# Block 0 of a sliding-window attention layer: values copied from SBUF to SBUF, or written to DRAM once and read back

## The chip, the cores and the metric

The kernel runs on one core of a Trainium2 chip. The core has five engines, each with its own queue of instructions in a fixed order: TensorE (PE, matmuls), VectorE (DVE), ScalarE (ACT), GpSimd (POOL) and SyncE (SP), which here issues the transfers. The transfers themselves are carried out by 16 DMA engines. SBUF is the core's memory of 128 partitions, PSUM the accumulators that PE writes, DRAM the chip's large memory. The metric is the time of one launch on the device, in microseconds (us), as the median of several runs.

## The reference

Four layers follow one another, A, B, A, B, on a sequence of 2048 positions with 512 features, 32 heads of 16. Each adds its result to x. Layer A is linear attention with a softmax feature map. Layer B, which the change touches, is attention over 8 earlier positions, two apart:

```python
W, dil = 8, 2
idx = pos[:, None] - off[None, :]          # off = 0, 2, ..., 14
kg = k[:, :, idx_c, :]                     # 8 keys for each position
vg = v[:, :, idx_c, :]                     # 8 values for each position
logits = einsum("bhsd,bhswd->bhsw", q, kg) * scale   # masked where idx < 0
attn = softmax(logits, axis=-1)
o = einsum("bhsw,bhswd->bhsd", attn, vg)   # then @ wo
```

x = x + A(layernorm(x)) and x = x + B(layernorm(x)), each twice, with the same weights the second time. All data are bf16.

## The kernel before, in words

The 2048 positions are worked on in four blocks of 512, b = 0 to 3. x stays in SBUF from beginning to end. A layer is a row of stages for each block, and the stages of different blocks, and of neighbouring layers, are interleaved, so that block 1 of a layer may be ahead of block 0.

Layer B of one block goes like this. The normalised x (xn) is transposed to xnT, with features on the partitions; for most blocks this is one DMA transpose that SP issues (line 451, "xnT<-xn"). Stage b1 (s_b1) multiplies xnT with WB (line 928) into q, k and v; four PSUM tiles each are copied to SBUF as QT, K and V (line 192 by ACT or line 190 by DVE). K and V have a rim of 16 columns with the last positions of the block before, which POOL copies (lines 954 to 970). Stage b2 forms the products of q with the eight shifted k (line 1026, DVE), sums them over the features of a head by matmuls with a 0/1 matrix (line 1033, PE), takes the exponential (line 1040, ACT), and sums and divides (lines 1049 to 1061). Stage b3 multiplies the attention weights PT with the values (pav, line 1088, DVE), sums over the window by matmuls (line 1097) and multiplies with the output weights WoB (line 520); lines 523 to 533 add x.

In the b3 stage the partitions stand for window offset and head, not for features. So V, which has features on the partitions, has to be spread: for each of the four feature groups dl = 0 to 3 and each of four window offsets g, a set of 32 rows of V (one for each head) is copied to the 32 partitions from 32 g on, each copy with its columns shifted by 2 g. The result is Vg, one tile for two dl. That makes sixteen copies of 32 rows (131.5 KB each) for a block. They are issued by vrep, one step for each dl, four copies in a step (line 995).

For b = 1, 2, 3 the step for dl = 0 first issues vwr (line 974): the whole V tile of the block is written to a DRAM buffer "vd" (528 KB), and the sixteen copies read from there ("Vg<-vd"). A copy can only be issued when the write has landed, so SP waits there. For b = 0 there is no write, and the copies read the V tile in SBUF itself ("Vg<-V").

The order in which each engine does its steps is written out by hand as one long list (_ORDER) of step names; _CHOICE says which copies go to DVE and which to ACT, and _SLOTS which buffer each tile gets. SP therefore issues its transfers in one fixed order, and an issue that waits holds all issues behind it. Each transfer takes the next of eight completion counters in turn, and its issue waits until the transfer before it on that counter has landed.

In SP's order, around the first layer B, stand: the first four copies of block 0; the write and the first four read-backs of block 1; the transpose of block 2; the other twelve read-backs of block 1; the transpose of block 3; the other twelve copies of block 0; the write of block 2 and its read-backs. In the second layer B stand: the transpose of block 1; eight copies of block 0; the transpose of block 2; the other eight copies of block 0; the transpose of block 3; then write and read-backs of block 1.

Of the kernel before, what the change touches and what calls it, by code (L numbers as in the profile page):

```python
# [19 lines left out]
H = 32  # L20
# [3 lines left out]
NB = 4  # L24
# [5 lines left out]
KVW = 16 + TB  # L30
VGW = 3 * KVW + TB + 8
# [98 lines left out]
class _Fast:  # L130
# [789 lines left out]
    def s_b1(self, L, b):  # L920
        nc, add = self.nc, self.step
        st = "b1_%d%d" % (L, b)
        T = {}
        def mm(i, c):
            xnT = self.xnT["B%d" % L, b]
            T[i, c] = pp = self.ps()
            for k in range(NB):
                nc.tensor.matmul(pp[:], lhsT=self.WB[:, k, i * D + c:(i + 1) * D:NB], rhs=xnT[:, :, k, :],  # L928
                                 start=(k == 0), stop=(k == NB - 1))

        def ev(i, c, dve):
            if i == 0:
                if (L, b) not in self.QT:
                    self.QT[L, b] = self.med([NB, TB], "QT")
                dst = self.QT[L, b][:, c, :]
            elif i == 1:
                ktile()
                dst = self.K[L, b][:, c, 16:KVW]
            else:
                vtile()  # L940
                dst = T["V"][:, c, 16:KVW]
            self.copy(dve, dst, T[i, c][:])

        def ktile():
            if (L, b) not in self.K:
                self.K[L, b] = self.med([NB, KVW], "K")

        def vtile():
            if "V" not in T:
                T["V"] = self.med([NB, KVW], "V")  # L950

        def halo():
            ktile()
            nc.gpsimd.tensor_copy(out=self.K[L, b][:, :, 0:16], in_=self.K[L, b - 1][:, :, TB:KVW])

        def kzero():
            ktile()
            nc.gpsimd.memset(self.K[L, b][:, :, 0:16], 0.0)

        def vzero():  # L960
            vtile()
            nc.gpsimd.memset(T["V"][:, :, 0:16], 0.0)

        def vhalo_in():
            vtile()
            nc.gpsimd.tensor_copy(out=T["V"][:, :, 0:16], in_=self.vh[L, b - 1][:])

        def vhalo_out():
            self.vh[L, b] = self.sm([NB, 16], "vh", BF16)
            nc.gpsimd.tensor_copy(out=self.vh[L, b][:], in_=T["V"][:, :, TB:KVW])  # L970

        def vwr():
            self.VD[L, b] = self.dram.tile([P, NB * KVW], BF16, name="vd%d%d" % (L, b))
            nc.sync.dma_start(out=self.VD[L, b][:], in_=T["V"][:].rearrange("p c t -> p (c t)"))

        def vrep(dl):
            if dl == 0:
                self.Vg[L, b] = {}
            if dl % 2 == 0:
                self.Vg[L, b][dl // 2] = self.big([2, NB * KVW], "Vg")  # L980
            if (L, b) in _OPT["v_dram"]:
                a = self.VD[L, b][dl:dl + 1, 2:3]
                src = bass.AP(a.tensor, a.offset, [[2, 4], [4 * NB * KVW, H], [1, VGW]])
                nc.sync.dma_start(out=self.Vg[L, b][dl // 2][:, dl % 2, 0:VGW], in_=src)
                return
            if dl == 0 and b:
                vwr()
            for g in (0, 2, 1, 3):
                if b:
                    a = self.VD[L, b][dl:dl + 1, 2 + 2 * g:3 + 2 * g]  # L990
                    src = bass.AP(a.tensor, a.offset, [[4 * NB * KVW, H], [1, VGW]])
                else:
                    a = T["V"][dl:dl + 1, 0:1, 2 + 2 * g:3 + 2 * g]
                    src = bass.AP(a.tensor, a.offset, [[4 * a.ap[0][0], H], [1, VGW]])
                nc.sync.dma_start(out=self.Vg[L, b][dl // 2][32 * g:32 * g + 32, dl % 2, 0:VGW], in_=src)

        if b:
            add(st + "v", "POOL", vhalo_in)
        else:
            add(st + "k", "POOL", kzero)  # L1000
            add(st + "v", "POOL", vzero)
        for i in range(3):
            for c in range(NB):
                add(st + "qkv"[i], "PE", mm, i, c)
                self.flex(st + "qkv"[i], ev, i, c)
        if b:
            add(st + "kh", "POOL", halo)
        if b < 3:
            add(st + "v", "POOL", vhalo_out)
        if (L, b) in _OPT["v_dram"]:  # L1010
            add(st + "v", "SP", vwr)
        for dl in range(4):
            add(st + "v", "SP", vrep, dl)
# [232 lines left out]
class _Layout:  # L1246
# [6 lines left out]
    def add(self, name, nelem, nbuf=1):  # L1253
        self.regions[name] = (self.off, nelem, nbuf)
        self.off += nelem * nbuf
        return self
# [568 lines left out]
```

## Time and profile before

| | |
|---|---|
| median of 3 runs | 327.89 us (327.71 to 328.19) |
| profiled execution | 328.31 us, its span 326.6 us |
| busy share of the span | PE 95%, DVE 93%, ACT 86%, POOL 8% |
| chain that ended last | PE 81%, ACT 8%, DMA 5%, DVE 3% |
| copies Vg<-V (block 0) | 32 of 131.5 KB, median 4.4 us to landing |
| copies Vg<-vd (blocks 1 to 3) | 96 of 131.5 KB, median 3.0 us to landing |
| writes vd<-V | 6 of 528.0 KB, median 3.1 us to landing |
| granted PE clock | 0.999 of full |

The profile comes from one execution, whose time (328.31 us) is a little above the median of the runs. Its span of 326.6 us begins with the first and ends with the last instruction; what lies around it belongs to the launch. PE and DVE are both busy nearly all the time, so the share of busy time alone doesn't say which of them sets the end at a given place. The chain does: it is followed back from the last instruction, at each step to what released it. "Line L928" is line 928 of the kernel. PEld is PE's loading of weights, which runs beside the matmuls.

In a list in order of time each row has its start and its length in us, the engine, and the operation; for SP the length is the time that the issuing took, not that of the transfer. "DMA to landing" is the time from issue until the data are there.

### The profile page before, as it was taken

What the parts mean: (1) busy time and instruction counts of PE and PEld (TensorE: products, weight loads), DVE (VectorE), ACT (ScalarE), POOL (GpSimd) and SP (SyncE); (2) the same over time, 40 slices, a digit from 0 to 9 for tenths busy, and PEclk for the clock granted to TensorE, in tenths of its full rate; (3) what the DMA queues carried; (4) which work ended last, traced back from release to release, by engine and by line L of the source; (5) the groups of instructions that cost most, each with busy time, mean ns of one, the idle gap of its engine ahead of it and who ended that gap; (6) DMA issues with size and microseconds to landing.
All of it is one profiled execution on the core that took longest, in us unless ns stands there. A gap on an engine that the chain in (4) does not pass through costs nothing.

```text
span 326.6 us, 8036 instructions
## 1 busy us (share of the span) xinstructions
PE 309.8 (95%) x3176; PEld 149.7 (46%) x3203; DVE 302.2 (93%) x439; ACT 279.2 (86%) x634; POOL 25.4 (8%) x50
## 2 busy tenths in 40 slices
PE   7999999999999999999999999979999999989873
PEld 3655456445454444443444455644544554433220
DVE  7998995998999999999989999699999999999993
ACT  5999988998898999899999999798999996676550
POOL 4000000000021002000000000000000208400000
PEclk9999999999999999999999999999999999999999
DMA  7980000014557889687540200042336976468632
GB/s 200 364 211 4 0 2 4 2 29 120 118 136 181 211 152 133 190 143 188 151 132 13 54 3 2 4 121 75 99 67 123 173 164 197 143 219 248 186 118 85
DMA packets 39404, 38.92 MB, mean 119 GB/s; under 512 B 24256, under 2 KB 33472, under 8 KB 39360
## 3 DMA queue, kind: packets, MB, share of 16 engines
q1 hardware_dynamic: 38832, 38.32, 47.3%
q8 instruction: 27, 0.44, 0.6%
q14 instruction: 17, 0.14, 0.2%
q10 hardware_dynamic: 528, 0.02, 0.1%
HBM read 23.43 MB, written 5.87 MB: 90 GB/s over the span
## 4 chain that ended last, share of the span: by engine, by line
PE 81%; ACT 8%; DMA 5%; DVE 3%; SPq 1%; issue 1%; DVEq 0%
PE ps L928 24%; PE ps L520 15%; PE ps L593 9%; PE ps L605 8%; PE ps L698 6%; PE ps L1097 4%; PE ps L1033 3%; ACT oT L192 3%; PE ps L668 2%; PE ps L460 2%; ACT Eq L706 2%; DMA xnT<-xn 2%; DMA wraw<-in_A_wqkv_dram 1%; PE ps L523 1%; PE ps L901 1%
## 5 line engine op out<-in xcount | busy, mean ns | idle before, releaser
L928 PE MATMUL ps<-xnT,WB 128*128 128x512 bf16 x384 | 87.5, 380 | 0.1
L1026 DVE TENSOR_TENSOR prod<-QT,K 128x4096 bf16<-128x4096 bf16 x32 | 72.5, 2290 | 0.3 <-ACT QT L192 0.2
L1088 DVE TENSOR_TENSOR pav<-PT,Vg 128x4096 bf16<-128x4096 bf16 (+1 forms) x34 | 72.0, 2161 | 0.4
L928 PEld LDWEIGHTS <-WB 128*128 128x128 bf16 x384 | 42.5, 114 | 42.6 <-issue 5.8
L520 PEld LDWEIGHTS <-oT 128*128 128x128 bf16 x256 | 23.9, 98 | 34.4 <-ACT oT L192 5.8
L192 ACT CAST oT<-ps 128x512 bf16<-128x512 f32 (+1 forms) x60 | 32.1, 586 | 8.4 <-PE ps L1097 7.0
L706 ACT ACTIVATE Eq<-ps 128x512 bf16<-128x512 f32 x64 | 34.0, 614 | 0.7 <-PE ps L698 0.5
L520 PE MATMUL ps<-WoB,oT 128*128 128x512 bf16 x122 | 32.1, 380 | 2.4 <-ACT oT L192 2.0
L599 ACT ACTIVATE Ek<-ps 128x512 bf16<-128x512 f32 x64 | 33.6, 621 | 0.3 <-PE ps L593 0.2
L698 PE MATMUL ps<-xnT,WA 128*128 128x512 bf16 x128 | 30.6, 380 | 0.6 <-DVE Eq L816 0.6
L540 ACT ACTIVATE sqd<-x 128x512 bf16<-128x512 bf16 x48 | 30.1, 643 | 0.5 <-DVE x L533 0.3
L593 PE MATMUL ps<-WA,xnT 128*128 128x512 bf16 x124 | 29.7, 379 | 0.8 <-DMA xnT<-xn 0.5
L605 PE MATMUL ps<-WA,xnT 128*128 128x512 bf16 x120 | 30.0, 379 | 0.5 <-issue 0.2
L520 PE MATMUL ps<-WoA,oT 128*128 128x512 bf16 x120 | 29.2, 379 | 0.4
L533 DVE SCALAR_TENSOR_TENSOR x<-ps,x 128x512 bf16<-128x512 f32 x38 | 25.3, 685 | 2.5 <-PE ps L520 2.4
L192 ACT CAST V<-ps 128x512 bf16<-128x512 f32 x31 | 17.5, 597 | 4.4 <-PE ps L928 4.3
L192 ACT CAST K<-ps 128x512 bf16<-128x512 f32 x31 | 17.9, 587 | 3.5 <-PE ps L928 3.4
L530 ACT ACTIVATE x<-ps 128x512 bf16<-128x512 f32 x26 | 15.2, 600 | 6.3 <-PE ps L523 6.3
L593 PEld LDWEIGHTS <-xnT 128*128 128x128 bf16 x128 | 12.1, 98 | 15.6 <-DMA xnT<-xn 0.9
L192 ACT CAST QT<-ps 128x512 bf16<-128x512 f32 x29 | 17.1, 592 | 2.5 <-PE ps L928 2.5
L651 DVE TENSOR_TENSOR Ek<-Ek,rk 128x4096 bf16<-128x4096 bf16 (+1 forms) x10 | 18.6, 1858 | 0.5 <-ACT rk L646 0.5
L446 ACT ACTIVATE xn<-x,nmr,rstd 128x512 bf16<-128x512 bf16 x23 | 18.2, 822 | 0.8 <-DVE nmr L435 0.6
(129 smaller groups left out, 433.2 us busy)
## 6 DMA issues: line engine op xcount, KB each, us to landing
Vg<-vd SPq DMA_DIRECT2D x96, 131.5 KB, 3.0
Vg<-V SPq DMA_DIRECT2D x32, 131.5 KB, 4.4
Prho<-rd SPq DMA_DIRECT2D x8, 512.0 KB, 5.1
vd<-V SPq DMA_DIRECT2D x6, 528.0 KB, 3.1
x<-in_A_x_dram SPq DMA_DIRECT2D x3, 512.0 KB, 6.8
WB<-in_B_wqkv_dram SPq DMA_DIRECT2D x3, 512.0 KB, 10.9
wraw<-in_A_wqkv_dram SPq DMA_DIRECT2D x4, 256.0 KB, 4.3
out_dram<-x SPq DMA_DIRECT2D x4, 256.0 KB, 2.3
```

The source lines that it names most:

```text
L192: self.nc.scalar.copy(out=out, in_=in_)
L520: nc.tensor.matmul(y[:], lhsT=oT[:, c, t * P:(t + 1) * P], rhs=Wo()[:, c, :], start=(c == 0), stop=(c == NB - 1 and not onpe))
L533: nc.vector.scalar_tensor_tensor(out=xb[:, t, :], in0=T[t][:], scalar=1.0, in1=xb[:, t, :], op0=ALU.mult, op1=ALU.add, **kw)
L540: nc.scalar.activation(out=sqd[:], in_=xb[:, t, :], func=ACT.Square, accum_out=T["ss"][:, t:t + 1])
L593: nc.tensor.matmul(pk[:], lhsT=xnT[:, t, k, :], rhs=self.WA[:, k, D:2 * D], start=(k == 0), stop=(k == NB - 1))
L599: nc.scalar.activation(out=T["E"][:, t, s, :], in_=T["k", t][:], func=ACT.Exp, scale=1.0 - 2.0 * s)
L605: nc.tensor.matmul(pv[:], lhsT=xnT[:, t, k, :], rhs=self.WA[:, k, 2 * D:3 * D], start=(k == 0), stop=(k == NB - 1))
L698: nc.tensor.matmul(pq[:], lhsT=self.WA[:, k, hb * P:(hb + 1) * P], rhs=xnT[:, :, k, :], start=(k == 0), stop=(k == NB - 1))
L706: nc.scalar.activation(out=self.Eq[L, b][s][:, :, hb, :], in_=T[hb][:].rearrange("p (t i) -> p t i", t=4), func=ACT.Exp, scale=1.0 - 2.0 * s)
L928: nc.tensor.matmul(pp[:], lhsT=self.WB[:, k, i * D + c:(i + 1) * D:NB], rhs=xnT[:, :, k, :], start=(k == 0), stop=(k == NB - 1))
L1026: nc.vector.tensor_tensor(out=pr[:], in0=QT[:, c:c + 1, :].to_broadcast([P, NW, TB]), in1=win, op=ALU.mult)
L1088: nc.vector.tensor_tensor(out=pv, in0=PT[:, :, lo:lo + n].unsqueeze(1).to_broadcast([P, NB, 2, n]), in1=vw, op=ALU.mult)
```

## The change: block 0 goes through DRAM too

In vrep, block 0 is treated as the other blocks are: its step for dl = 0 first writes the V tile to a DRAM buffer of its own, and all sixteen copies read that buffer. This holds for both layers B. The order of the steps, the buffers and the engines of all other work stay the same.

```diff
@@ def vrep(dl), in s_b1
-            if dl == 0 and b:
+            if dl == 0:
                 vwr()
             for g in (0, 2, 1, 3):
-                if b:
-                    a = self.VD[L, b][dl:dl + 1, 2 + 2 * g:3 + 2 * g]
-                    src = bass.AP(a.tensor, a.offset, [[4 * NB * KVW, H], [1, VGW]])
-                else:
-                    a = T["V"][dl:dl + 1, 0:1, 2 + 2 * g:3 + 2 * g]
-                    src = bass.AP(a.tensor, a.offset, [[4 * a.ap[0][0], H], [1, VGW]])
+                a = self.VD[L, b][dl:dl + 1, 2 + 2 * g:3 + 2 * g]
+                src = bass.AP(a.tensor, a.offset, [[4 * NB * KVW, H], [1, VGW]])
                 nc.sync.dma_start(out=self.Vg[L, b][dl // 2][32 * g:32 * g + 32, dl % 2, 0:VGW], in_=src)
```

SP has two issues more (one write in each layer B); 32 copies change their source from SBUF to DRAM. The write function that vrep calls is this:

```python
def vwr():
    self.VD[L, b] = self.dram.tile([P, NB * KVW], BF16, name="vd%d%d" % (L, b))
    nc.sync.dma_start(out=self.VD[L, b][:], in_=T["V"][:].rearrange("p c t -> p (c t)"))
```

## The prediction, made before the changed kernel was timed

> **What bounds the kernel now.** I read three views: the page's engine shares and its chain, then the chain in order of time, then SP's queue in order of time. First the page: TensorE (PE) is busy for 95% of the span and carries 81% of the chain that ended last.
>
> ```profile
> span 326.6 us, 8036 instructions
> PE 309.8 (95%) x3176; PEld 149.7 (46%) x3203; DVE 302.2 (93%) x439; ACT 279.2 (86%) x634; POOL 25.4 (8%) x50
> PE 81%; ACT 8%; DMA 5%; DVE 3%; SPq 1%; issue 1%; DVEq 0%
> ```
>
> The change touches layer B, which runs twice: from about 84 to 150 us, and from 238 us to the end. The chain in order of time (start, length, what), from the first of them:
>
> ```profile
> 107.69 1.41 PE ps L1033 x24
> 109.09 1.85 PE ps L928 x8
> ...
> 134.00 5.32 PE ps L928 x24
> 139.34 0.59 ACT K L192
> ...
> 140.97 1.41 ACT xn L446 x2
> 142.41 5.73 DMA xnT<-xn
> 148.14 0.05 issue
> 148.19 0.39 PE ps L593
> ```
>
> The reader is to see that from 107.69 to 139.3 the chain has matmuls alone, one behind another, then a short piece of ACT, one transpose by DMA, and PE again. So a moment that PE loses at 109 is not made good before 148: each of these steps begins when the one before it ends. The rows left out are of the same kind.
>
> SP issues every transfer, in one fixed order, and an issue that waits holds all that stand behind it. Its queue (start, time in issue, line, what) in the stretch of the first block 0:
>
> ```profile
> 95.36 2.47 SPq L995 DMA_DIRECT2D Vg<-V  x4
> 99.10 0.38 SPq L974 DMA_DIRECT2D vd<-V  x1
> 101.85 1.71 SPq L995 DMA_DIRECT2D Vg<-vd  x4
> 103.73 2.37 SPq L451 DMA_TRANSPOSE xnT<-xn  x1
> 106.14 7.63 SPq L995 DMA_DIRECT2D Vg<-vd  x12
> 116.16 1.32 SPq L451 DMA_TRANSPOSE xnT<-xn  x1
> 117.53 9.00 SPq L995 DMA_DIRECT2D Vg<-V  x12
> 126.65 0.51 SPq L974 DMA_DIRECT2D vd<-V  x1
> 134.32 5.63 SPq L995 DMA_DIRECT2D Vg<-vd  x12
> 142.41 1.96 SPq L451 DMA_TRANSPOSE xnT<-xn  x1
> ```
>
> The four rows from 95.36 to 103.73 decide the case. They are block 0's first four copies, block 1's write, block 1's first four read-backs and the transpose that brings block 2's input, xnT. Between 99.10 and 101.85 SP does nothing: it waits for the write to land before it may read it back.
>
> **Part 1, first layer B: a write ahead of four copies.** Now the four copies at 95.36 read the SBUF tile V, and wait for nothing but V. After the change a write of 528 KB is issued at 95.36 and the copies wait for it. The trace's rows of the same sequence, write, four read-backs, write, are these, from block 2 and 3 of the second layer B:
>
> ```profile
> 281.72 0.34 SPq L974 DMA_DIRECT2D vd<-V  x1
> 284.50 1.70 SPq L995 DMA_DIRECT2D Vg<-vd  x4
> 286.31 0.35 SPq L974 DMA_DIRECT2D vd<-V  x1
> ```
>
> So the wait costs 284.50 - 281.72 = 2.78 us, the copies themselves get cheaper (1.70 us for four against 2.47), and the second write comes 286.31 - 281.72 = 4.59 us after the first, at 95.36 + 4.59 = 99.95. It stands at 99.10 today, where it waits for block 1's last V (the ACT row below), so it is late by 0.85 us.
>
> ```profile
> 98.44 0.59 ACT L192 CAST V<-ps 128x512 bf16<-128x512 f32 x1
> ```
>
> Then the second write has to land. How long the writes at 99.10 and at 286.31 took from issue to landing:
>
> ```profile
> L974 SPq DMA_DIRECT2D vd<-V x1: 384/384/384, 99.1 to 99.1; - x1
> DMA to landing us min/median/max: 2.7/2.7/2.7
> ...
> L974 SPq DMA_DIRECT2D vd<-V x1: 352/352/352, 286.3 to 286.3; - x1
> DMA to landing us min/median/max: 3.3/3.3/3.3
> ```
>
> I take 3.3, as the write at 286.31 is the one that stands directly behind four read-backs, as block 1's will; at 99.10 the last copy was issued 1.3 us before. The lower end is 2.7. So block 1's read-backs start at 99.95 + 3.3 + 0.05 = 103.30 (lower end 102.70), and the transpose, which follows them by 103.73 - 101.85 = 1.88 us, is issued at 105.18 (lower end 104.58), late by 1.45 (0.85) us. Its own input doesn't hold it: the xn that it reads is made by ACT at 101.77 to 102.60.
>
> When is that late? The transpose at 103.73 took 4.8 us to land, at 108.53. In the program's order its first reader is the weight load of the L928 matmul behind the 24 matmuls of L1033, which began at 109.02:
>
> ```profile
> L451 SPq DMA_TRANSPOSE xnT<-xn x1: 2367/2367/2367, 103.7 to 103.7; - x1
> DMA to landing us min/median/max: 4.8/4.8/4.8
> ...
> 101.77 0.83 ACT L446 ACTIVATE xn<-x,nmr,rstd 128x512 bf16<-128x512 bf16 x1
> 109.02 1.44 PEld L928 LDWEIGHTS <-WB 128*128 128x128 bf16 x8 [0.42 <-issue]
> ```
>
> There are 0.49 us to spare. After the change it lands at 105.18 + 4.8 = 109.98 (lower end 109.38), and PE stands still for 109.98 - 109.02 = 0.96 us (lower end 0.36), at a place where it never stood before. Behind that weight load on PE's queue is everything up to 139; nothing there can pass it.
>
> [...]
>
> **Part 2, the twelve copies at 117.53, and what is behind them.** They get cheaper: 9.00 us now, 5.63 us for the twelve read-backs at 134.32. I cost this at nothing. What stands behind them is block 2's write at 126.65, which then waits for block 2's V, and its read-backs at 134.32, which can start earlier as their write lands with less ahead of it. Their reader is block 2's pav on DVE, the x4 at 155.43:
>
> ```profile
> 155.43 8.90 DVE L1088 TENSOR_TENSOR pav<-PT,Vg 128x4096 bf16<-128x4096 bf16 x4
> ```
>
> One thing on the chain may profit: the transpose at 142.41, 5.73 us to landing against 4.8 for the one at 103.73. With fewer transfers ahead of it it could be quicker. But PE ended its work before it only 0.45 us ahead of that landing, so the gain has an upper end of about 0.4 us:
>
> ```profile
> 148.19 1.04 PE L593 MATMUL ps<-WA,xnT 128*128 128x512 bf16 x3 [0.45 <-DMA xnT<-xn]
> ```
>
> I take nothing, because the four read-backs that go out right behind this transpose, in whose company it runs, stay where they are.
>
> **Part 3, second layer B.** Here block 0 issues eight copies, then a transpose:
>
> ```profile
> 246.26 5.00 SPq L995 DMA_DIRECT2D Vg<-V  x8
> 252.35 2.89 SPq L451 DMA_TRANSPOSE xnT<-xn  x1
> ...
> L451 SPq DMA_TRANSPOSE xnT<-xn x1: 2893/2893/2893, 252.4 to 252.4; - x1
> DMA to landing us min/median/max: 4.6/4.6/4.6
> ...
> 257.91 2.75 PE L928 MATMUL ps<-xnT,WB 128*128 128x512 bf16 x12
> ```
>
> After the change: 246.26 + 2.78 for the write, then eight read-backs at 1.70 / 4 = 0.43 us each, ends at 252.44, against 251.26 now. The transpose waits until 252.35 in any case, for ACT; so it is late by 0.1 to 0.3 us and lands by 257.3. Its first reader is the fifth of the twelve matmuls at 257.91, at 258.77 (2.75 / 12 is about 0.22 each). There is 1.4 us of cover: nothing. Block 0's other eight copies here get cheaper, ahead of a transpose that waits for ACT as well: nothing.
>
> **Part 4, the V tile gets free sooner.** Its buffer is held now until the last copy from it has landed, after 126.5; then until the write has, about 98.1. Its next user is the xn of block 0 for the following layer A, which is made behind the transpose at 142.41. Nothing. The work of PE, DVE, ACT and POOL doesn't change by an instruction; SP has two issues more.
>
> **Sum.** 0.96 + 0 + 0 + 0 = about +0.95 us on the profiled execution's 328.31 us. That is 0.42 above the median of the runs, 327.89; on the median it gives 328.8.
>
> **Rivals.** (a) *The transpose is in time after all: not slower.* The cover of 0.49 us holds if the late issue is made good in flight. Transposes here land in 4.2 to 5.7 us; at 4.2 with the lower end of the issue (104.58) it lands at 108.78, ahead of 109.02, and there is no stall; with the up to 0.4 us of part 2, the time is 327.5 to 328.1. It decides when write plus transpose take under 7.1 us from 99.95 to landing (less the 1.9 of the read-backs), against 8.1 by the rows that I took. For it: both durations vary by half a microsecond. Against: both would have to be at their low ends. Chance 0.22.
> (b) *The write lands much later: a longer stall.* The write at 126.65 took until after 134, because copies were queued ahead of it. If block 1's write sees even a fifth of that delay behind block 0's four read-backs, 1 us more, the stall is 2 us and the time 329.9; the range of this case is 329.3 to 330.5. For it: four transfers are in flight when it starts. Against: at 286.31 four were too, and it took 3.3. Chance 0.13.
> (c) *The DMA engines, not the queue, are relieved and the run gets faster.* Copies that read SBUF and write SBUF go away, and the twelve take 3.4 us less. For it: the 9.00 and 5.63 rows. Against: no reader of these copies is on the chain, and a relief beyond the 0.4 us at 148 has no place to show. 327.2 or less; chance 0.04.
> The change does what it says: SP's list in the changed program has one write more per layer B and all 128 copies reading DRAM.
>
> **How the numbers follow.** The forecast has 0.61: a stall that leaves 0.4 to 1.2 us after what is given back at 148, so 328.3 to 329.1, and 328.8 as the likeliest. 0.2%, about what a measurement of this kernel can tell from no change, is 0.66 us: slower means above 328.55, faster below 327.23. Of the forecast's 0.61 some 0.47 lies above 328.55 and 0.14 inside; (b) is slower; (a) is inside but for 0.01; (c) is faster. That is slower 0.60, same 0.35, faster 0.05. The range from 327.8 to 329.6 leaves out the fast half of (a), (c), and the slower half of (b), about 2 in 10.
>
> **What the changed profile would show.** Right: in SP's queue a write at 95.4, its four read-backs about 2.8 us later, block 1's write at 99.9 to 100.0, and the transpose at 104.6 to 105.2; an idle time of about 1 us of PE or its weight load ahead of L928 near 109, released by the DMA of xnT; everything after it later by that much, and the chain with a DMA piece there that it lacks today; no new wait near 258. Wrong: no such wait (rival a); or the same wait at 109 with the end unmoved, which would mean that some engine later on had slack to give that I read as a chain without any.

## The result, and the profile after

The changed kernel takes 329.27 us (median of 5 runs, 329.11 to 329.84), where the kernel before took 328.18 us beside it on the same chip (5 runs, 327.71 to 328.25). The ratio is 1.0043, with a 95% interval of 1.0028 to 1.0057: slower by 1.09 us. The profiled execution of the changed kernel took 329.27 us as well. The changed kernel's lines from vrep on have numbers lower by four: L991 is L995 of before, L1029 is L1033. One of the ten executions of the first-four kernel below (334.22 us) fell in a slower state of the chip and is left out of its median and its ratio.

The page of the changed kernel, its span and the engine shares of the chain that ended last:

```profile
span 327.5 us, 8031 instructions
...
PE 81%; ACT 8%; DMA 6%; DVE 3%; SPq 1%; issue 1%; DVEq 0%
```

The span has grown by 0.9 us, and the share that moved is the chain's DMA, from 5% to 6%. SP's queue of the changed kernel in order of time (start, time in issue, line, what):

```profile
95.63 0.39 SPq L974 DMA_DIRECT2D vd<-V  x1
98.34 1.71 SPq L991 DMA_DIRECT2D Vg<-vd  x4
100.16 0.36 SPq L974 DMA_DIRECT2D vd<-V  x1
103.42 1.70 SPq L991 DMA_DIRECT2D Vg<-vd  x4
105.28 3.07 SPq L451 DMA_TRANSPOSE xnT<-xn  x1
...
143.58 1.84 SPq L451 DMA_TRANSPOSE xnT<-xn  x1
145.47 3.30 SPq L991 DMA_DIRECT2D Vg<-vd  x4
```

Block 0's write is at 95.63; its read-backs start 2.71 us later; block 1's write is at 100.16 in place of 99.10, and its read-backs come 3.26 us after it. So the transpose of block 2 is issued at 105.28, where it was at 103.73. PE of the kernel before in order of time, at the step that reads this transpose first, and under it PE of the changed kernel (the brackets give the idle time before, and what ended it):

```profile
107.61 1.48 PE L1033 MATMUL ps<-prod,indQK 128*32 128x512 bf16 x24
109.03 1.92 PE L928 MATMUL ps<-xnT,WB 128*128 128x512 bf16 x8
```

```profile
107.89 1.48 PE L1029 MATMUL ps<-prod,indQK 128*32 128x512 bf16 x24
110.20 1.92 PE L928 MATMUL ps<-xnT,WB 128*128 128x512 bf16 x8 [0.83 <-DMA xnT<-xn]
...
149.56 1.04 PE L593 MATMUL ps<-WA,xnT 128*128 128x512 bf16 x3 [0.65 <-DMA xnT<-xn]
...
259.28 2.75 PE L928 MATMUL ps<-xnT,WB 128*128 128x512 bf16 x12
```

PE now stands still for 0.83 us ahead of the first reader of that transpose. The wait at 149.56 was there before, with 0.45 us. At 259.28, the same place in the second layer B, there is none. The chain in order of time has the piece that it lacked:

```profile
103.48 1.80 PE ps L520 x8
105.28 4.87 DMA xnT<-xn
110.15 0.05 issue
110.20 1.92 PE ps L928 x8
...
142.15 1.41 ACT xn L446 x2
143.56 0.03 ACT x L530
143.58 5.93 DMA xnT<-xn
```

How late each place is can be followed from row to row. A step well ahead of the change, in the layer before, shows what the two profiled executions differ by from the start. Before (this step and the last piece of the chain):

```profile
69.02 0.44 DVE rho L801
...
321.22 0.69 DVE x L533
```

After:

```profile
69.30 0.44 DVE rho L801
...
322.59 0.69 DVE x L533
```

The changed kernel's profile is 0.28 us late before the change acts. At the L928 matmuls it is 110.20 - 109.03 = 1.17 us late. Of that 0.83 is the idle time, and 0.06 comes from an overlap that is gone: before, by the two rows above, these eight started 0.06 us ahead of the end of the 24. At the transpose of 143.58 it is still 1.17 us late. At the L593 matmuls it is 149.56 - 148.19 = 1.37 us late: the transpose took 5.93 us in place of 5.73, which adds 0.20. At the last step of the chain it is still 1.37, which is 1.09 us net of the start.

That this equals the difference of the medians is partly chance, since these are two single executions. What follows the last step, up to the end of the span, took 4.2 us where it took 4.7 before (321.22 + 0.69 from 326.6, and 322.59 + 0.69 from 327.5), so the span is only 0.9 us longer. The chain doesn't show what made this difference.

### The profile page after: what moved, and what is told of

Its sections match the earlier page's. It is cut to its first block, busy times and chain, and to the rows that moved or that the text cites. A ratio compares the mean times of both kernels' runs of the same rounds, so it can differ in the third digit from the quotient of the medians.

```text
span 327.5 us, 8031 instructions
## 1 busy us (share of the span) xinstructions
PE 310.6 (95%) x3176; PEld 150.0 (46%) x3203; DVE 302.5 (92%) x439; ACT 279.1 (85%) x634; POOL 28.3 (9%) x50
## 4 chain that ended last, share of the span: by engine, by line
PE 81%; ACT 8%; DMA 6%; DVE 3%; SPq 1%; issue 1%; DVEq 0%
PE ps L928 25%; PE ps L520 14%; PE ps L593 9%; PE ps L605 8%; PE ps L698 6%; PE ps L1093 4%; DMA xnT<-xn 3%; PE ps L1029 3%; ACT oT L192 3%; PE ps L668 2%; ACT Eq L706 2%; PE ps L460 2%; DMA wraw<-in_A_wqkv_dram 2%; PE ps L901 1%; PE ps L523 1%
## 5 line engine op out<-in xcount | busy, mean ns | idle before, releaser
L928 PE MATMUL ps<-xnT,WB 128*128 128x512 bf16 x384 | 87.5, 380 | 0.9 <-DMA xnT<-xn 0.8
L928 PEld LDWEIGHTS <-WB 128*128 128x128 bf16 x384 | 42.5, 114 | 43.5 <-issue 5.4
L593 PE MATMUL ps<-WA,xnT 128*128 128x512 bf16 x124 | 29.7, 379 | 1.0 <-DMA xnT<-xn 0.6
L593 PEld LDWEIGHTS <-xnT 128*128 128x128 bf16 x128 | 12.1, 98 | 15.8 <-DMA xnT<-xn 1.1
```

The source lines that it names most:

```text
L593: nc.tensor.matmul(pk[:], lhsT=xnT[:, t, k, :], rhs=self.WA[:, k, D:2 * D], start=(k == 0), stop=(k == NB - 1))
```

## The experiments

The theory is that of the prediction: SP waits once more for a write, the transpose behind that wait comes late, and PE stands still for it. Its rivals were that the twelve changed copies do it, by their traffic, that the second layer takes a part, and that any write to DRAM costs by itself. Each kernel was timed in five rounds, beside the kernel before on the same chip; the ratios are against that. The kernel before had a median of 328.60 us beside the first four kernels, 328.75 beside the last-twelve kernel of the first layer alone, the transpose between, the two writes and the read-backs ahead, and 328.52 beside the last two. So the ratios can be compared, the times in us only within a group.

**One layer at a time.** First only the first layer B goes through DRAM for block 0, then only the second.

```diff
-            if dl == 0 and b:
+            if dl == 0 and (b or L == 0):
...
-                if b:
+                if b or L == 0:
```

> Only the first layer B takes block 0's values through DRAM; the second copies from SBUF as before. Theory (PE stands still near 110 us because the transpose of block 2 is issued 1.3 us late behind the wait for the write): all of the loss, +0.9 to +1.2 us on the kernel before, with the idle time of 0.8 us ahead of L928 near 110. Rival (every copy through DRAM costs something, by DMA work added): about half in each layer, +0.5 us.

```diff
+            if dl == 0 and (b or L == 1):
...
+                if b or L == 1:
```

> Only the second layer B takes block 0's values through DRAM. Theory: nothing, -0.2 to +0.2 us, since the transpose behind the eight read-backs there has more than a microsecond of cover. Rival (added DMA work): about +0.5 us.

The first layer alone: 329.32 us, ratio 1.0029 (1.0016 to 1.0043). The second alone: 328.51 us, 0.9999 (0.9989 to 1.0010). PE of the first-layer kernel, and under it PE of the second-layer kernel, at the same place:

```profile
107.56 1.48 PE L1033 MATMUL ps<-prod,indQK 128*32 128x512 bf16 x24
109.63 1.92 PE L928 MATMUL ps<-xnT,WB 128*128 128x512 bf16 x8 [0.60 <-DMA xnT<-xn]
```

```profile
107.92 1.48 PE L1033 MATMUL ps<-prod,indQK 128*32 128x512 bf16 x24
109.33 1.92 PE L928 MATMUL ps<-xnT,WB 128*128 128x512 bf16 x8
```

The whole loss that can be measured, about 0.95 us by the ratio, is in the first layer, where the idle time is (0.60 us in this execution, where 0.8 was expected), and the second layer costs nothing that five rounds can tell.

**The first four copies, or the last twelve.** In the one kernel only the step for dl = 0 reads DRAM, and the other twelve copies read SBUF as before; in the other only the twelve read DRAM, and the write is issued ahead of them. Both layers.

```diff
-            if dl == 0 and b:
+            if dl == 0:
...
-                if b:
+                if b or dl == 0:
```

> In both layers the write stands ahead of the first four copies and only these four read DRAM; the other twelve copy from SBUF as before. Theory (the wait for the write ahead of the first four): the same as with all sixteen, +0.9 to +1.2 us, with the same idle time near 110. Rival (the twelve later ones and what moves behind them matter): +0.4 us or less.

```diff
-            if dl == 0 and b:
+            if dl == (0 if b else 1):
...
-                if b:
+                if b or dl:
```

> In both layers the first four copies read SBUF as before; the write stands ahead of the second step, and the other twelve read DRAM. Theory: no idle time near 109, so the time of the kernel before, -0.4 to +0.2 us, although as many bytes are written to DRAM and three quarters of the copies read it. Rival (added DMA work): +0.7 us or more.

The first four alone give 329.49 us, 1.0027 (1.0015 to 1.0040): this is the loss of the first layer again, with twelve copies untouched. PE there:

```profile
108.17 1.48 PE L1033 MATMUL ps<-prod,indQK 128*32 128x512 bf16 x24
110.44 1.92 PE L928 MATMUL ps<-xnT,WB 128*128 128x512 bf16 x8 [0.79 <-DMA xnT<-xn]
```

The last twelve alone give 328.94 us, 1.0018 (0.9996 to 1.0040), where no change was expected; one execution of 332.51 us widens the interval, which leaves that open. In the first layer nothing is idle at 109. But in the second layer the moved wait holds a transpose that the expectation didn't count. SP there:

```profile
246.24 2.44 SPq L995 DMA_DIRECT2D Vg<-V  x4
248.73 0.59 SPq L974 DMA_DIRECT2D vd<-V  x1
252.63 1.71 SPq L995 DMA_DIRECT2D Vg<-vd  x4
254.44 3.04 SPq L451 DMA_TRANSPOSE xnT<-xn  x1
```

and PE:

```profile
257.89 1.03 PE L928 MATMUL ps<-xnT,WB 128*128 128x512 bf16 x4
260.63 1.89 PE L928 MATMUL ps<-xnT,WB 128*128 128x512 bf16 x8 [1.71 <-DMA xnT<-xn]
```

Here the write stands behind four copies instead of ahead of them. It takes 3.9 us instead of 2.7 until it may be read, the transpose goes out at 254.44 where it went out at 252.35, and PE waits 1.71 us. The late issue is only a small part of that: with the 4.6 us that this transpose took before it would have landed at 259.04, some 0.1 us after PE was ready at 258.92. The rest is its flight, which took 6.1 us here. So the wait for the write delays a transpose at a second place too, where the full change did no harm, but most of PE's idle time there comes from a longer flight whose cause is open. The profiled execution (329.89 us) is 0.95 us above this kernel's median, so how large that wait is in the other runs stays open.

So the last twelve were tried again in the first layer only, with the second as before.

```diff
+            if dl == (1 if (L, b) == (0, 0) else 0) and (b or L == 0):
...
+                if b or (L == 0 and dl):
```

> In the first layer B alone: the first four copies read SBUF as before, the write stands ahead of the second step, the other twelve read DRAM; the second layer B is as before. Theory (where the wait stands decides, and ahead of the twelve nothing on PE's path stands behind it): no idle time near 109, -0.3 to +0.2 us on the kernel before. Rival (the write and the DRAM copies cost by themselves): +0.5 us or more.

328.40 us, 0.9998 (0.9988 to 1.0009). A write and twelve read-backs more in the first layer cost nothing that can be measured when no transpose stands close behind the wait. Neither the twelve nor a write as such is the cause.

**The transpose taken from behind the wait.** The full change, but in the first layer B block 1's write is a step of its own, and block 2's transpose is issued between it and its read-backs. All transfers of the change are there; only that order differs.

```diff
-            if dl == 0:
+            if dl == 0 and (L, b) != (0, 1):
                 vwr()
...
-        if (L, b) in _OPT["v_dram"]:
+        if (L, b) in _OPT["v_dram"] or (L, b) == (0, 1):
             add(st + "v", "SP", vwr)
```

In _ORDER the steps on SP then stand as: block 1's write, the transpose of block 2, block 1's first read-backs.

> All of the change is kept; in the first layer B alone, block 2's transpose is moved in SP's order to stand between block 1's write and its first four read-backs. Theory (only the place of this transpose behind two waits for a write costs): it is issued as soon as its xn is there, near 102.7 us, lands near 107.5, the idle time near 110 is gone and the time is that of the kernel before, -0.3 to +0.3 us, with two writes more and 32 copies through DRAM. Rival (added DMA work): still +0.7 us or more.

328.42 us, 0.9997 (0.9987 to 1.0006): the loss is gone. SP:

```profile
95.34 0.39 SPq L974 DMA_DIRECT2D vd<-V  x1
98.06 1.71 SPq L991 DMA_DIRECT2D Vg<-vd  x4
99.88 0.36 SPq L974 DMA_DIRECT2D vd<-V  x1
102.62 1.72 SPq L451 DMA_TRANSPOSE xnT<-xn  x1
104.43 8.90 SPq L991 DMA_DIRECT2D Vg<-vd  x16
```

and PE:

```profile
107.60 1.48 PE L1029 MATMUL ps<-prod,indQK 128*32 128x512 bf16 x24
109.02 1.92 PE L928 MATMUL ps<-xnT,WB 128*128 128x512 bf16 x8
```

The transpose goes out at 102.62, 1.1 us earlier than in the kernel before (103.73, where its xn was made at 102.60), and nothing waits at 109. But it is no faster than the kernel before either: PE had not been waiting for this transpose there, so being earlier than needed wins nothing.

**The suspected wait made longer.** The full change, and in the first layer block 0's V is written twice, the first time to a buffer that nothing reads.

```diff
             if dl == 0:
+                if (L, b) == (0, 0):
+                    vx = self.dram.tile([P, NB * KVW], BF16, name="vx")
+                    nc.sync.dma_start(out=vx[:], in_=T["V"][:].rearrange("p c t -> p (c t)"))
                 vwr()
```

> All of the change is kept; in the first layer B, block 0's V is written to DRAM twice, the first time to a buffer that nobody reads, so that the wait ahead of the first four read-backs gets longer by what a second write of 528 KB adds (an estimate of 1.2 to 2.5 us). Theory: the idle time of PE near 110 grows by as much, to 2 to 3.3 us, and all of it reaches the end: +2.2 to +3.5 us on the kernel before. Rival (later engines have slack and take part of it back): the idle time grows but the end moves by less than 1.7 us.

334.31 us, 1.0182 (1.0162 to 1.0201): 5.6 us slower than the kernel before by the medians, about 6 by the ratio, and well beyond the 2.2 to 3.5 us that were expected. SP:

```profile
95.77 0.39 SPq L989 DMA_DIRECT2D vx<-V  x1
96.21 0.41 SPq L974 DMA_DIRECT2D vd<-V  x1
99.82 1.72 SPq L994 DMA_DIRECT2D Vg<-vd  x4
101.66 0.36 SPq L974 DMA_DIRECT2D vd<-V  x1
105.17 1.70 SPq L994 DMA_DIRECT2D Vg<-vd  x4
107.03 2.93 SPq L451 DMA_TRANSPOSE xnT<-xn  x1
```

The read-backs behind the two writes wait 4.05 us (95.77 to 99.82), against 2.71 behind the one write of the changed kernel, so the second write adds 1.34 us here; the 1.2 to 2.5 us put on it in advance were my estimate, with no run named for it. The transpose is 1.75 us later than in the changed kernel, and it took 6.4 us to land, against 4.9. PE, in order of time, and then the windows around it (the columns are length, busy us and count of PE, PEld, DVE, ACT and POOL, the granted PE clock, the DMA share and GB/s):

```profile
108.03 1.48 PE L1032 MATMUL ps<-prod,indQK 128*32 128x512 bf16 x24
113.44 3.29 PE L928 MATMUL ps<-xnT,WB 128*128 128x512 bf16 x8 [3.94 <-DMA xnT<-xn]
```

```profile
108.00:109.40 1.40, 1.40 (x25) 0.55 (x24) 1.26 (x2) 1.40 (x5) 0.70 (x1) 1.00 0.86 145
109.50:113.40 3.90, 0.01 (x2) 0.00 (x0) 3.80 (x4) 1.00 (x4) 0.00 (x0) 0.93 1.00 209
113.44:116.70 3.26, 3.25 (x12) 1.06 (x16) 0.38 (x3) 0.99 (x3) 0.00 (x0) 0.56 0.92 258
116.70:119.00 2.30, 2.30 (x18) 1.03 (x18) 0.71 (x3) 1.89 (x6) 0.00 (x0) 1.00 0.55 141
```

PE stands still for 3.94 us, some 1.5 us of it for the slower transpose, and then the same eight matmuls that took 1.92 us take 3.29, at a granted clock of 0.56 instead of 1.00. The sum is 3.94 + 1.37 = 5.3 us; the rest to 5.6 is within the spread of the runs. The direction and the place are as the theory says. The size holds two things that it didn't have: the slower transpose, whose cause is open, and the clock.

**The transpose at 142.** The 5.7 us of this one transpose were left unexplained by the prediction but for "the company" of the four read-backs behind it. Two kernels start from the kernel before and take these four away from their place: ahead of the transpose, or behind the next one. A third is the kernel with the transpose between, together with the later place.

SP's order in the kernel before (first line) and in the "ahead" and "later" kernels:

```diff
-  ... transpose (142) | four read-backs | transpose (150) ...
+  ... four read-backs | transpose (142) | transpose (150) ...
+  ... transpose (142) | transpose (150) | four read-backs ...
```

> The kernel before (block 0 copies from SBUF), with one step moved: the last four read-backs of block 2 in the first layer B stand ahead of the transpose at 142 us and not right behind it. Theory (this transpose takes 5.7 us to land for the company of these four): it lands in 4.3 to 4.8 us, PE's idle time of 0.45 us near 148 goes, -0.3 to -0.5 us on the kernel before. Rival (its length has another cause): no change, -0.1 to +0.1 us.

> The kernel before, with the last four read-backs of block 2 in the first layer B moved behind the next transpose (150 us), so that nothing goes out behind the transpose at 142 us for eight microseconds. Theory (its 5.7 us come from the four transfers right behind it): it lands in 4.2 to 4.7 us, PE's idle time of 0.45 us near 148 goes, -0.3 to -0.5 us on the kernel before. Rival (another cause): it still takes 5.7 us, and the time stays within 0.1 us.

> All of the change, with block 2's transpose between block 1's write and read-backs, and the last four read-backs of block 2 behind the transpose at 150 us. Theory: as the kernel before with the same move, -0.3 to -0.5 us. Rival: no gain over the kernel with the first of the two moves alone, within 0.2 us of the kernel before.

Ahead: 328.93 us, 1.0005 (0.9994 to 1.0015). The transpose took 5.9 us to land; but the read-backs were issued until 141.93, 0.77 us before it, and no read-back of the kernel before landed in less than 2.2 us, so by that measure the last ones were still in flight, and this one tells nothing apart. Later: 328.56 us, 1.0007 (0.9996 to 1.0019). The transpose between and the four later, together: 328.46 us, 0.9996 (0.9985 to 1.0007). The transpose of the "later" kernel:

```profile
L451 SPq DMA_TRANSPOSE xnT<-xn x1: 1952/1952/1952, 143.2 to 143.2; - x1
...
DMA to landing us min/median/max: 5.6/5.6/5.6
```

Nothing of the four is behind it any more, and it takes 5.6 us against 5.7, as it does with the transpose between and the four later. PE's wait behind it is 0.28 and 0.36 us in these two, against 0.45: less than the times can tell. The theory of the company falls.

## Why the prediction was right, point by point

The forecast of 328.8 us, slower by 0.95 us, had the right sign and about the right size: 1.09 us were measured. Part of the closeness is luck: the stall was put 0.13 us too long, and the 0.20 and 0.06 us of the longer flight and the lost overlap stood at nothing in the sum.

- *Part 1, the wait.* Right. The prediction had 2.78 us from write to read-back, 3.3 us for the landing of block 1's write and the transpose at 105.18. The rows show 2.71, 3.2 and, net of the 0.28 us at the start, 105.00. The stall was put at 0.96 us and measured at 0.83. Taking the row that stands behind four read-backs, 3.3 us, and not that of the write at 99.10, 2.7, was what made the size right. That the late issue causes the loss is shown from both sides: it goes when the transpose alone is moved out from behind the wait, and grows when the wait does.
- *Its passing on to the end.* Right: each later step of the chain is late by at least as much; only what follows its last step was 0.5 us shorter in the profiled execution.
- *Part 2, nothing at 142.* The forecast was no change, and it took 0.20 us more; the reason given was wrong. The transpose took 5.93 us and not less, but not because of the four read-backs: without them it takes 5.6.
- *Part 3, nothing in the second layer.* Right; the second layer alone has a ratio of 0.9999. The last-twelve kernel shows that it was not safe by much: with the wait four copies later, PE stands still there, though mostly for a longer flight.
- *Part 4 and the rest of the traffic: nothing.* The 0.9998 of the twelve copies in the first layer agrees; V's tile was not tried by itself.
- *Rivals.* (a), in time after all, would have needed block 1's write at 2.7 us and the transpose at 4.2; they took 3.2 and 4.9. (b), a write landing far later, didn't come: 3.2 us. (c), relief of the DMA engines, didn't come either: with the loss removed, the kernel with copies through DRAM is as fast as the one with copies from SBUF, not faster (0.9997), though SP issues the twelve in 6.35 us in place of 9.00.

Neither the 0.20 nor the 0.06 us can be told from the medians alone, whose interval is 1.0028 to 1.0057. But the longer flight at 143.58 is no accident of one execution: PE waits 0.65, 0.68 and 0.66 us for that transpose in the changed, the first-layer and the first-four kernel, which all lose at 109, against 0.45 in the kernel before and the second-layer kernel. Why is open; the two-writes kernel, which loses more, has 0.43.

## What to carry to other kernels

In this kernel a round trip through DRAM was paid at the issuing queue, by an unrelated transfer that stood next behind the wait: it was issued 1.55 us later (105.28 against 103.73), and PE stood still for 0.83 us. In another kernel, look for that transfer, take its landing and the start of its first reader, and the slack between them is what the wait may cost. Here cheaper copies brought nothing where no one waited for them (0.9998), and an order in which the write is issued, then the unrelated transfer, then the read-back, hid the wait (0.9997). When such a change moves a wait, check every layer or block in which the same code stands, since what follows it in the queue differs.

## What the runs showed of the hardware that I had not expected

**A wait of 3.94 us cost more than itself.** Idle times of PE of 0.83 us (changed kernel) and 1.71 us (last twelve) left the eight matmuls behind them at 1.92 and 1.89 us, at a granted clock of 1.00. After the 3.94 us of the two-writes kernel they took 3.29 us: the granted clock was 0.93 in the window of the idle time (109.50 to 113.40), 0.56 in that of the matmuls (113.44 to 116.70), and 1.00 again in the next (116.70 to 119.00). From what length on an idle time does this, these three don't show.

**The flight of a write differed with what stood ahead of it.** In the changed kernel the 528 KB took 2.7 us at 95.63, with no copies just ahead; 3.2 us behind four read-backs, at 100.16; 4.5 us behind twelve read-backs, at 126.66. In the kernel before, behind twelve copies from SBUF, the write at 126.65 took 7.5 us, and the read-backs had to wait until 134.32, 7.7 us after the issue.

**A transpose that was slow at one place in every profile.** The same transpose of 512 columns lands in 4.2 to 4.9 us at the other places of the kernel before and of the changed kernel. The one that leads into the following layer A took 5.6 to 6.0 us in all twelve profiles, whether it was issued at 142.3 or at 148.2, and with or without the four read-backs. In the packets of the trace, one of 16 KB on the queue that the page calls "instruction" lies in this flight, both in the kernel before and in the changed kernel. In the kernel before it begins 3.0 us after the issue, and 20 of the transpose's own packets of 256 bytes, which begin from 0.2 us behind it on, take 1.2 to 1.5 us each (start and length in us, the longest of the small ones):

```
kernel before:       instruction packet 145.43 0.94    20 packets of the transpose from 145.64, 1.53
```

In the kernel before no packet over 0.9 us lies in the transposes of 4.2 to 4.4 us. In the changed kernel the instruction packet begins 3.9 us after the issue (147.48, 0.93 us), without such small packets behind it (none over 0.12 us), and the flight is as long. But the transpose near 87 us has one 4.0 us after its issue in the kernel before (91.16, 0.95 us), and lands in 4.7 us. So this is a coincidence in time and not a shown cause; moving that packet or the transpose against it was not tried. What it is worth at this place is bounded by PE's wait there, 0.45 us in the kernel before.
